# The first batch's prologue in two halves of the heads, its loads issued in another order, in a fused attention and feed-forward kernel

## The chip, the cores and the metric

The kernel runs on one core of a Trainium2 chip. The metric is the device time of one execution in microseconds (us). Engines are called as in the profile: PE (TensorE matmuls) and PEld (its weight loads), DVE (VectorE), ACT (ScalarE), POOL, SP; SPq and ACTq are the instruction queues of SP and ACT where they issue transfers (DMAs).

## The reference

For 8 batches of 8 heads (576 positions, head width 64) the keys and values are first summed into 32 memory slots per head, with softmax weights over the slots; the queries then attend to these 32 slots; the result, 4608 rows of 512, passes a two-layer feed-forward net with 2048 hidden units. All is float32, and the two weight matrices arrive as float64 words.

```python
a = softmax(phi)                        # over the 32 slots; phi: (8, 8, 576, 32)
k_m = einsum('bhsm,bhsd->bhmd', a, k)
v_m = einsum('bhsm,bhsd->bhmd', a, v)
attn = softmax(q @ k_m.T / 8)           # over the 32 slots
x = (attn @ v_m) as (4608, 512)
h = x @ w_in
out = (h * sigmoid(h)) @ w_out
```

## The kernel before

**The work of a batch.** Heads are laid out as two groups of four: group p (0 or 1), written g in tile layouts, takes columns or partitions 64 p to 64 p + 63 of a tile, and r (0 to 3) runs over the four heads of a group. A batch takes `phi` (loaded as `e`, 4 full chunks of 128 positions, and `er`, the last 64), subtracts the maximum, takes the exponential, multiplies it onto keys and values (`e_mm`; the tile `kv{c}` is chunk c, `kr` the last 64 positions; a column of ones gives the softmax sum beside), divides (`kvn`), transposes (`f_tr`, into `kvT`), and multiplies the keys with the queries (`f_scores`). The scores are copied (`f_copy`), turned by PE so that the slots lie along the free axis (`f_turn`), and go through maximum, subtraction, exponential, sum, reciprocal and product (`f_max`, `f_sub`, `f_exp`, `f_sum`, `f_norm`). They are turned back (`f_back`) and split into a rounded high part and the rest (`f_high`, `f_low`), so that matmuls in the fast float32 format keep the precision. The values are multiplied into `w_in` beforehand (`p_mm`, split by `p_split`), so that the hidden layer is one product of attention weights with this matrix (`ffn1`). Then come silu, a split and the second layer (`main_step`), for 16 chunks of 128 hidden units.

**The weights in the first batch.** They arrive as 64-bit words (`w_load`, 512 KB a half). `w_conv` makes float32 of them in steps: `p` and `c` on ACT (L172, L174), `s` and `a` on DVE (L176, L178), and for `w_out` `h` on ACT (L180) and `l` on DVE (L182). I0, O0 and I1 are the first chunks of `w_in`, `w_out` and the second of `w_in`; I0 and O0 come in two halves, 0 and 1.

**The order of the work.** The prologue of batch 0 is written out by hand (L1153 to L1251). Inside it PE, DVE, ACT and SP each run their instructions in the order in which the code names them. `keep_warm` adds matmuls without use so that PE is not idle. Behind the prologue a table of events puts each step at a slot of a chunk; the change does not touch that table, and the order of each engine behind the prologue is as it was.

**The halves before.** `f_scores(u)`, `f_copy(u)` and `f_turn(u)` work on half u of the query positions (288 each) for all eight heads; so both halves need the whole `kvT`, and with it all keys and values. Maximum to split then run for `u = 0`, `u = 1`, and the leftover 64 positions go with `u = 1`.

**The loads before.** `load_phi(0)` issues two parts on SP and one on ACT, 576 KB together. ACT then issues the four chunks of `kv` (516 KB each) and `kr` (258 KB); SP issues I0's first half, the two query halves (576 KB each), I0's second half, O0, I1 and the next weights. On SP every load from the first of I0 on is made to wait for the landing of the load that stands `DEEP = 5` places ahead in the code (`few=True`).

**The counters.** Each load reports its landing on one of eight counters, DMAHW0 to DMAHW7, which the framework hands out in turn in the order in which its scheduler places the loads. A load that gets a counter which another holds waits, in the queue of its engine, until that other load has landed.

Of the kernel before, what the change touches and what calls it, by code (L numbers as in the profile page):

```python
# [10 lines left out]
F32 = mybir.dt.float32  # L11
# [8 lines left out]
P = 128  # L20
# [6 lines left out]
CW = 256  # L27
# [21 lines left out]
def attn_ffn_kernel(  # L49
# [179 lines left out]
    def load_kv(b, cs=range(FULLC)):  # L229
        queue = nc.scalar if b == 0 else None  # L230
        ts = at[b].setdefault("kv", [])
        for c in cs:
            tag = f"q{c - 2}" if b > 2 and c > 1 else f"kv{c}"
            t = sb.tile([P, 2, NR, KVW], F32, tag=tag, name=f"kv{b}_{c}", bufs=1)
            load(t.rearrange("p g r f -> p (g r f)"), kv[b, :, c * KVC : (c + 1) * KVC], queue=queue)
            ts.append(t)
        if cs[0]:
            return
        t = sb.tile([P, NR, KVW], F32, tag="kr", name=f"kr{b}", bufs=1)
        load(t.rearrange("p r f -> p (r f)"), kv[b, :, FULLC * KVC :], queue=queue)  # L240
# [243 lines left out]
    first = {}  # L484
    UW = (2 * HM, 2 * HM + P)

    def f_tr():
        pt = ps.tile([P, 512], F32, tag="acc", name="firstt", bufs=NI)
        t = sb.tile([P, 2, NR, M], F32, tag="kvT", name="kvT0", bufs=2)
        at[0]["kvT"] = t  # L490
        for kind in range(2):
            nc.tensor.transpose(
                pt[:, P * kind : P * (kind + 1)], kvn[:, kind].rearrange("p g d -> p (g d)"), ident
            )
        nc.vector.tensor_copy(t[:, 0].rearrange("p r m -> p (r m)"), pt[:, :P])
        first["vt"] = t, pt

    def f_vt():
        t, pt = first["vt"]
        nc.scalar.copy(t[:, 1].rearrange("p r m -> p (r m)"), pt[:, P : 2 * P])  # L500

    def f_scores(u):
        if u == 0:
            t = [ps.tile([P, 512], F32, tag="acc", name=f"firsts{p}", bufs=NI) for p in range(2)]
        else:
            h = ps.tile([P, 2, 512], F32, tag="h", name="firsts", bufs=1)
            t = [h[:, p] for p in range(2)]
        kvT, q = at[0]["kvT"], at[0]["q", u]
        for r in range(NR):
            for p in range(2):  # L510
                nc.tensor.matmul(
                    t[p][M * r : M * (r + 1), :HALF],
                    kvT[D * p : D * (p + 1), 0, r],
                    q[D * p : D * (p + 1), r],
                    start=True, stop=True, skip_group_check=True,
                )
        first["st", u] = t if u == 0 else h

    def f_copy(u):
        if u == 0:  # L520
            first["left"] = sb.tile([P, P], F32, tag="mx", name="sleft", bufs=1)
        t = first["main", u] = sb.tile([P, 2, 2 * P], F32, tag=f"kv{u}", name=f"sT{u}", bufs=1)
        left = first["left"].rearrange("p (g h f) -> p g h f", g=2, h=2)[:, :, u]
        st = first["st", u]
        if u:
            nc.scalar.copy(t, st[:, :, : 2 * P])
            nc.scalar.copy(left, st[:, :, 2 * P : HALF])
# [36 lines left out]
    def f_max(u):  # L564
        nc.vector.tensor_reduce(
            f_part(u, "mx", 2 * S // M), f_groups(first["ps", u][:, : UW[u]]), op=ALU.max, axis=AX.X
        )

    def f_sub(u):
        nc.vector.tensor_tensor(  # L570
            f_groups(f_sc(u)), f_groups(first["ps", u][:, : UW[u]]), f_bc(f_part(u, "mx", 2 * S // M), u),
            op=ALU.subtract,
        )

    def f_exp(u):
        nc.scalar.activation(f_sc(u), f_sc(u), AF.Exp, scale=SCALE)

    def f_sum(u):
        sm = f_part(u, "sm", 2 * S // M)
        nc.vector.tensor_reduce(sm, f_groups(f_sc(u)), op=ALU.add, axis=AX.X)  # L580
# [22 lines left out]

    def f_to(x, u):
        v = at[0][x].rearrange("p g (h f) -> p g h f", h=2)
        return v[:, :, u, : 2 * P] if u < 2 else v[:, :, :, 2 * P :]

    def f_high(u):
        if "ahi" not in at[0]:
# [544 lines left out]
    with in_order(DVE, ACT) as last:  # L1154
        load_phi(0)
        nc.scalar.activation(tiny[:, :1], ident[:, :1], AF.Exp)
        load_kv(0)
        for c in LOADS.split():
            if c[0] == "Q":
                load_q(0, int(c[1]), True)  # L1160
            elif c[0] == "L":
                load_next(True)
            else:
                w_load((c[0], 0), int(c[1]), True)
        keep_warm(idle, 10)
        phi_max(0, (0,))
        phi_allmax(0, (0,))
        phi_max(0, (1,))
        keep_warm(idle, 3)
        phi_sub(0, (0,))  # L1170
        phi_allmax(0, (1,))
        phi_sub(0, (1,))
        for p in range(2):
            phi_exp(0, (p,))
        keep_warm(idle, 2)
        e_mm(0)
# [31 lines left out]
        w_conv(O0, 0, "c")
        keep_warm(spare, 3)
        bg = p_mm(0, 0, CW, False)  # L1210
        keep_warm(spare, 5)
        p_split(0, 0, CW, bg, (0,))
        w_conv(I1, None, "p")
# [7 lines left out]
        w_conv(O0, 0, "h")  # L1221
        f_low(1)
# [172 lines left out]
```

## Time and profile before

| | us |
|---|---|
| device time, median of 3 runs (lowest, highest) | 675.97 (675.60, 676.06) |
| the profiled execution's own time | 676.14 |
| its span, first to last instruction | 674.4 |
| PE busy | 664.5 |
| DVE busy | 518.7 |
| ACT busy | 370.2 |

So 1.74 us of the profiled execution lie outside its span. The times in the views count from the span's start. A row of the timeline gives the start and the length of a piece of work, the engine, the line in the code, the operation and its tiles, and in square brackets how long the engine was idle before and what ended that. A matmul of float32 operands shows as two records.

### The profile page before, as it was taken

To read this page: it belongs to the slowest core of one execution; us is meant where nothing else is said; L and a number is where in the kernel's file an instruction comes from. 1 tells how busy PE (TensorE), PEld (TensorE's weight loads), DVE (VectorE), ACT (ScalarE), POOL (GpSimd) and SP (SyncE) were. 2 spreads that over 40 slices of the span, in tenths; PEclk is the share of its full clock that TensorE was granted. 3 is DMA by queue.
4 is the path that set the end of the run, shared out by engine and by line. 5 is a ranking of instruction groups with operands and counts; after the bars stand their busy time and mean duration, and the time that the engine had idled before them with its cause. 6 is when DMAs were issued, how large, how long until landed. Compare 5 with 4: busy or idle time off the path is not lost.

```text
span 674.4 us, 14536 instructions
## 1 busy us (share of the span) xinstructions
PE 664.5 (99%) x5792; PEld 588.7 (87%) x5792; DVE 518.7 (77%) x1092; ACT 370.2 (55%) x686; POOL 0.7 (0%) x6
## 2 busy tenths in 40 slices
PE   7999999999999999999999999999999999999997
PEld 3588778887869998999988999899997999889996
DVE  3997899889958599878877688877877667867653
ACT  3878684534545556654645546564654646554441
POOL 0000000000000000000000000000000000000000
PEclk9999999999999999999999999999999999999999
DMA  9989985225251562253420534216430304300001
GB/s 340 366 329 298 313 308 184 91 92 172 93 188 38 185 205 79 79 201 131 153 94 17 185 121 163 69 47 229 157 126 33 87 2 157 115 27 18 32 1 48
DMA packets 37907, 93.92 MB, mean 139 GB/s; under 512 B 4688, under 2 KB 21456, under 8 KB 34256
## 3 DMA queue, kind: packets, MB, share of 16 engines
q1 hardware_dynamic: 36816, 90.22, 38.6%
q10 hardware_dynamic: 1024, 2.77, 1.1%
q8 instruction: 46, 0.75, 0.5%
q14 instruction: 21, 0.17, 0.1%
HBM read 77.22 MB, written 15.73 MB: 138 GB/s over the span
## 4 chain that ended last, share of the span: by engine, by line
PE 87%; DVE 2%; ACT 1%; issue 1%; DVEq 0%; ACTq 0%
PE sum L895 36%; PE h L856 23%; PE acc L746 9%; PE h L701 5%; PE lsum L979 5%; PE bg L649 3%; PE accleft L746 2%; PE bg L382 1%; PE h L335 1%; PE bg L335 1%; PE pacc L649 1%; DVE wf L814 0%; DVE kept L836 0%; ACT kept L835 0%; PE lsum L1001 0%
## 5 line engine op out<-in xcount | busy, mean ns | idle before, releaser
L856 PE MATMUL h<-aparts,pm 128*128 128x288 f32 x1152 | 168.5, 295 | 0.0
L856 PEld LDWEIGHTS h<-aparts,pm 128*128 128x128 f32 x1152 | 157.4, 189 | 0.5
L870 ACT ACTIVATE gbuf<-h 128x512 f32<-128x512 f32 x96 | 57.3, 597 | 117.1 <-PE h L856 113.8
L895 PE MATMUL sum<-wo_hi,aparts 128*128 128x256 f32 x384 | 102.4, 289 | 0.0
L895 PE MATMUL sum<-kept,aparts 128*128 128x256 f32 x576 | 100.2, 283 | 0.0
L895 PE MATMUL sum<-wo_lo,aparts 128*128 128x256 f32 x384 | 100.1, 282 | 0.0
L875 DVE TENSOR_TENSOR gbuf<-gbuf 128x256 f32<-128x256 f32 x96 | 40.6, 423 | 69.2 <-ACT gbuf L870 68.8
L884 ACT ACTIVATE aparts<-gbuf 128x512 fp32r<-128x512 f32 x86 | 54.4, 633 | 62.0 <-DVE gbuf L879 62.0
L895 PEld LDWEIGHTS sum<-kept,aparts 128*128 128x128 f32 x576 | 82.6, 191 | 0.0
L895 PEld LDWEIGHTS sum<-wo_hi,aparts 128*128 128x128 f32 x384 | 72.8, 190 | 9.8 <-ACT gleft L872 7.5
L886 DVE TENSOR_TENSOR gparts<-gbuf,aparts 128x512 fp32r<-128x512 f32 x86 | 59.6, 693 | 19.7 <-ACT aparts L884 19.6
L895 PE MATMUL sum<-wo_hi,gparts 128*128 128x256 f32 x384 | 73.2, 282 | 0.0
L895 PEld LDWEIGHTS sum<-wo_lo,aparts 128*128 128x128 f32 x384 | 73.2, 191 | 0.0
L746 PE MATMUL acc<-wo_hi,gparts 128*128 128x512 f32 x256 | 72.1, 395 | 0.0
L895 PE MATMUL sum<-kept,gparts 128*128 128x256 f32 x288 | 65.6, 282 | 0.0
L895 PEld LDWEIGHTS sum<-wo_hi,gparts 128*128 128x128 f32 x384 | 59.4, 190 | 0.0
L701 PEld LDWEIGHTS h<-aparts,pm 128*128 128x128 f32 x372 | 51.8, 188 | 6.3 <-issue 2.5
L701 PE MATMUL h<-aparts,pm 128*128 128x288 f32 x372 | 55.8, 299 | 0.5 <-DVE aparts L612 0.5
L746 PEld LDWEIGHTS acc<-wo_hi,gparts 128*128 128x128 f32 x256 | 46.1, 188 | 10.1 <-issue 1.0
L874 ACT ACTIVATE aparts<-gbuf 128x384 fp32r<-128x384 f32 x96 | 50.4, 525 | 0.0
L895 PEld LDWEIGHTS sum<-kept,gparts 128*128 128x128 f32 x288 | 47.9, 190 | 0.0
L885 DVE TENSOR_TENSOR gparts<-gbuf,aparts 128x384 fp32r<-128x384 f32 x86 | 47.4, 551 | 0.0
(226 smaller groups left out, 947.7 us busy)
## 6 DMA issues: line engine op xcount, KB each, us to landing
win<-win_saved SPq DMA_DIRECT2D x24, 1024.0 KB, 4.9
kv<-in_kv SPq DMA_DIRECT2D x28, 516.0 KB, 5.0
q<-in_q SPq DMA_DIRECT2D x16, 576.0 KB, 6.2
raw<-in_w_in SPq DMA_DIRECT2D x14, 512.0 KB, 7.8
raw<-in_w_out SPq DMA_DIRECT2D x6, 1024.0 KB, 6.9
win_saved<-win SPq DMA_DIRECT2D x4, 1024.0 KB, 8.7
phi<-in_phi SPq DMA_DIRECT2D x7, 576.0 KB, 8.0
out<-oo SPq DMA_DIRECT2D x26, 128.0 KB, 1.8
```

The costliest lines, as they stand in the source:

```text
L649: nc.tensor.matmul((bg[p][M * r : M * (r + 1)] if beside else bg[M * r : M * (r + 1), p, :w]).rearrange("p (k f) -> p k f", f=P), kvT[D * ...
L701: nc.tensor.matmul(h[:, hf, :HALF], wt[:, p, fs], a[:, p, hf * HALF : (hf + 1) * HALF], start=n[hf] == 0, stop=n[hf] == 5, skip_group_chec ...
L746: nc.tensor.matmul(acc[key], gt[:, cs], wt[:, fc], start=fc == 0 and n == 0, stop=fc == NFC - 1 and n == 2)
L856: nc.tensor.matmul(h[:, i, :HALF], wt[:, p, f : f + P], a[:, p], start=n == 0, stop=n == 5)
L870: nc.scalar.activation(gbuf[:, :MAIN].rearrange("p (i f) -> p i f", i=2), h[:, :, :w], AF.Silu)
L874: nc.scalar.activation(hi[:, :3], g[:, 1:4], AF.Copy)
L875: nc.vector.tensor_tensor(g[:, 4:6], g[:, :1].broadcast_to([P, 2, P]), g[:, 1:3], op=ALU.subtract)
L884: nc.scalar.activation(hi[:, 3:], g[:, 4:], AF.Copy)
L885: behind(nc.vector.tensor_tensor(lo[:, :3], g[:, 1:4], hi[:, :3], op=ALU.subtract).ins, s4)
L886: last_split.append(nc.vector.tensor_tensor(lo[:, 3:], g[:, 4:], hi[:, 3:], op=ALU.subtract))
L895: nc.tensor.matmul(sums[bank][:, place * Q : (place + 1) * Q], gt[:, k], wt, start=bank not in begun, stop=True, skip_group_check=True,)
L979: nc.tensor.matmul(sums[k], part[gt][:, 2 * i + k], wt[:, fc], start=n == 0 and i == 0 and m == 0, stop=True, skip_group_check=True,)
```

## The change

- **Loads.** `load_kv0(g)` and `load_q0(g)` load keys and values, and the queries, of one group of heads: 258 KB for a chunk of `kv`, 129 KB for `kr` and 288 KB for a half of the positions of `q`. Group 0 of `kv` goes on ACT's queue, all the rest on SP's. The code names `kv` of group 0, `q` of group 0, `kv` of group 1, I0's first half, `q` of group 1, I0's second half, and then the other weights as before. Only I0's second half and what follows it is still tied to the landing of an earlier load by `few`.
- **Order of computing.** The new `f_sums(p)` and `f_div(p)` take the place of `e_mm(0)` for the two groups one after the other. `f_tr`, `f_vt`, `f_scores`, `f_copy` and `f_turn` now work on one group of heads for all query positions. Group 0 is turned, and group 1 summed, before the maximum of group 0.
- **Softmax.** `f_sum` holds only the sums; `f_rec` takes the reciprocal of both halves together. `f_norm(0)` stands behind `f_sum(1)`.
- **Conversions.** I0's first half is converted behind `f_sub(0)`, its second `s` and `a` ahead of `f_sum(1)`, `p_mm(0, 0)` moves ahead of `f_norm(0)`, and I1's step `p` behind O0's `h`.
- **Buffers.** The copied scores lie in `gbuf` and not in the first two `kv` tiles.

```diff
+    def load_kv0(g, few=False):
+        queue = None if g else nc.scalar
...
+        for c in range(FULLC):
+            f = c * KVC + g * n
+            load(at[0]["kv"][c][:, g].rearrange("p r f -> p (r f)"), kv[0, :, f : f + n], few, queue)
+        load(at[0]["kr"][rows(g)].rearrange("p r f -> p (r f)"), kv[0, rows(g), FULLC * KVC :], few, queue)
...
+    def f_sums(p):
...
+        for c in range(FULLC):
+            for r in range(NR):
+                nc.tensor.matmul(
+                    pt[M * r : M * (r + 1), :KVW],
+                    e[:, p, c, M * r : M * (r + 1)],
+                    kvt[c][:, p, r],
+                    start=c == 0, stop=False, skip_group_check=True,
+                )
...
+    def f_div(p):
+        pt = first["pt", p]
+        rs = sb.tile([P, 1], F32, tag="rs", name="rs", bufs=2)
+        nc.vector.tensor_scalar(rs, pt[:, 2 * D : KVW], EPS, None, op0=ALU.add)
+        nc.vector.reciprocal(rs, rs)
+        src = pt[:, : 2 * D].rearrange("p (k d) -> p k d", k=2)
+        nc.vector.tensor_scalar(kvn[:, :, p], src, rs, None, op0=ALU.mult)
...
-        load_kv(0)
-        for c in LOADS.split():
...
+        load_kv0(0)
+        load_q0(0)
+        load_kv0(1)
+        w_load(I0, 0)
+        load_q0(1)
+        w_load(I0, 1, True)
...
-        e_mm(0)
-        w_conv(I0, 0, "pc")
-        keep_warm(idle, 3)
-        f_tr()
-        f_vt()
-        w_conv(I0, 0, "s")
-        keep_warm(idle, 2)
-        f_scores(0)
-        f_scores(1)
-        f_copy(0)
-        w_conv(I0, 0, "a")
-        f_turn(0)
-        f_copy(1)
-        f_max(0)
-        f_turn(1)
-        f_sub(0)
+        f_sums(0)
+        f_div(0)
+        keep_warm(idle, 3)
+        f_tr(0)
+        f_vt(0)
+        keep_warm(idle, 1)
+        f_scores(0)
+        f_copy(0)
+        keep_warm(idle, 1)
+        f_sums(1)
+        f_div(1)
+        f_turn(0)
+        f_tr(1)
+        f_vt(1)
+        f_max(0)
+        f_sub(0)
+        w_conv(I0, 0, "pc")
+        keep_warm(idle, 4)
+        f_scores(1)
+        f_exp(0)
+        w_conv(I0, 0, "sa")
+        f_copy(1)
+        f_turn(1)
         spare = ps.tile([P, 512], F32, tag="acc", name="spare", bufs=NI)
-        keep_warm(spare, 3)
-        f_exp(0)
+        keep_warm(spare, 6)
         w_conv(I0, 1, "pc")
+        f_sum(0)
         f_max(1)
         f_sub(1)
         f_exp(1)
         nc.scalar.activation(tiny[:, :1], ident[:, :1], AF.Silu)
-        keep_warm(spare, 13)
-        f_sum(0)
+        w_conv(I0, 1, "sa")
+        bg = p_mm(0, 0, CW, False)
+        keep_warm(spare, 3)
+        f_sum(1)
+        f_rec()
         f_norm(0)
-        w_conv(I0, 1, "sa")
         f_back(0)
-        f_sum(1)
...
```

How the rows of the engines stand, at three places. First ACT's own queue at the start, before (the names in square brackets are what a row waits for; `kv_c` is chunk c):

```order
L88 DMA kv_0_101<-in_kv 128x1032
L88 DMA kv_1_103<-in_kv 128x1032
L88 DMA kv_2_105<-in_kv 128x1032
L88 DMA kv_3_107<-in_kv 128x1032
L88 DMA kr_109<-in_kv 128x516 [waits DMAHW1_49]
L322 ACTIVATE phi_96<-phi_96 128x512 [waits DVE_49]
```

The same place now, where these are the loads of group 0:

```order
L88 DMA kv_0_101<-in_kv 128x516 [waits DMAHW2_49]
L88 DMA kv_1_102<-in_kv 128x516 [waits DMAHW4_49]
L88 DMA kv_2_103<-in_kv 128x516 [waits DMAHW5_49]
L88 DMA kv_3_104<-in_kv 128x516 [waits DMAHW7_49]
L88 DMA kr_105<-in_kv 64x516 [waits DMAHW0_49]
L342 ACTIVATE phi_96<-phi_96 128x512 [waits DMAHW1_49,DVE_49]
```

Each of the five loads of group 0 has become half as large, and each of them now waits for a counter, where one of five did. They stand ahead of the exponential of `phi` (L322, now L342) in the same queue, as before.

SP's queue at the start, now (`phi`, then queries and keys; `raw` are weights):

```order
L88 DMA phi_96<-in_phi 128x512
L88 DMA phi_96<-in_phi 128x128
L88 DMA q_0_111<-in_q 64x1152
L88 DMA q_1_113<-in_q 64x1152
L88 DMA kv_0_101<-in_kv 128x516
L88 DMA kv_1_102<-in_kv 128x516
L88 DMA kv_2_103<-in_kv 128x516
L88 DMA kv_3_104<-in_kv 128x516 [waits DMAHW0_49]
L88 DMA kr_105<-in_kv 64x516 [waits DMAHW1_49]
L88 DMA raw<-in_w_in 128x4x128 [waits DMAHW3_49]
L88 DMA q_0_111<-in_q 64x1152 [waits DMAHW6_49]
L88 DMA q_1_113<-in_q 64x1152 [waits DMAHW1_49]
```

Counters 1 to 7 go to the first seven of these rows in turn, counter 0 to the `phi` part on ACT; the eighth and ninth row take 0 and 1 again. ACT's five loads got theirs behind these: the counters that they wait for are held by the small `phi` part (2), `q_1` of group 0 (4), and `kv_0` (5), `kv_2` (7) and `kv_3` (0) of group 1. Before, SP's queue held, behind `phi`, I0's first half, which waited for the first `kv` chunk.

DVE before, from the division to the maximum of half 1 (`rs` and `kvn` divide, `fmx` and `fsc` are `f_max` and `f_sub`; L176 and L178 convert I0's first half):

```order
L353 TENSOR_SCALAR rs<-first_168 128x1
L353 TENSOR_SCALAR rs<-first_169 128x1
L355 RECIPROCAL rs<-rs 128x1 x2
L361 TENSOR_SCALAR kvn<-first_168,rs 128x2x64
L495 COPY kvT_224<-firstt 128x128
L176 TENSOR_SCALAR win_72<-win_72 128x512
L530 COPY sT_252<-firsts_233 128x256
L178 ISA win_72<-raw,win_72 128x1024
L565 TENSOR_REDUCE fmx<-firstu 128x16
L570 TENSOR_TENSOR fsc<-firstu,fmx 128x512
L565 TENSOR_REDUCE fmx<-firstu 128x20
```

DVE now, from the division of group 1 on:

```order
L529 TENSOR_SCALAR rs<-first_226 128x1
L530 RECIPROCAL rs<-rs 128x1
L532 TENSOR_SCALAR kvn<-first_226,rs 128x2x64
L544 COPY kvT_204<-firstt 64x128
L614 TENSOR_REDUCE fmx<-firstu 128x16
L619 TENSOR_TENSOR fsc<-firstu,fmx 128x512
L176 TENSOR_SCALAR win_72<-win_72 128x512
L178 ISA win_72<-raw,win_72 128x1024
L628 TENSOR_REDUCE fsm<-fsc 128x16
L614 TENSOR_REDUCE fmx<-firstu 128x20
```

I0's two conversion steps and `f_sum(0)` (L628) now stand between the maximum of half 0 and that of half 1, and a second division and a second copy of `kvT` stand ahead of both.

More of the change, by code (lines that the diff above doesn't have):

```diff
@@ L241, in load_kv, with load_q0 @@
         at[b]["kr"] = t
+    def load_kv0(g, few=False):
+        queue = None if g else nc.scalar
+        if g == 0:
+            at[0]["kv"] = [
+                sb.tile([P, 2, NR, KVW], F32, tag=f"kv{c}", name=f"kv0_{c}", bufs=1) for c in range(FULLC)
+            ]
+            at[0]["kr"] = sb.tile([P, NR, KVW], F32, tag="kr", name="kr0", bufs=1)
+        n = NR * KVW
+        for c in range(FULLC):
+            f = c * KVC + g * n
+            load(at[0]["kv"][c][:, g].rearrange("p r f -> p (r f)"), kv[0, :, f : f + n], few, queue)
+        load(at[0]["kr"][rows(g)].rearrange("p r f -> p (r f)"), kv[0, rows(g), FULLC * KVC :], few, queue)
+    def load_q0(g, few=False):
+        for hf in range(2):
+            if g == 0:
+                at[0]["q", hf] = sb.tile([P, NR, HALF], F32, tag=f"q{hf}", name=f"q0_{hf}", bufs=1)
+            d = slice(D * g, D * (g + 1))
+            load(at[0]["q", hf][d].rearrange("p r s -> p (r s)"), qT[0, hf, d], few)
     def load_q(b, hf, few=False):
@@ L485, in attn_ffn_kernel @@
     UW = (2 * HM, 2 * HM + P)
-    def f_tr():
+    def f_sums(p):
+        e, er, kvt, kr = (at[0][k] for k in ("e", "er", "kv", "kr"))
+        pt = first["pt", p] = ps.tile([P, 512], F32, tag="acc", name=f"first{p}", bufs=NI)
+        for c in range(FULLC):
[6 more added lines that the diff above has]
+                )
+        for r in range(NR):
+            nc.tensor.matmul(
+                pt[M * r : M * (r + 1), :KVW],
+                er[rows(p), M * r : M * (r + 1)],
+                kr[rows(p), r],
+                start=False, stop=True, skip_group_check=True,
+            )
@@ L488, in f_tr @@
+    def f_div(p):
[5 more added lines that the diff above has]
+        nc.vector.tensor_scalar(kvn[:, :, p], src, rs, None, op0=ALU.mult)
+    def f_tr(p):
         pt = ps.tile([P, 512], F32, tag="acc", name="firstt", bufs=NI)
-        t = sb.tile([P, 2, NR, M], F32, tag="kvT", name="kvT0", bufs=2)
@@ L490, in f_tr @@
-        at[0]["kvT"] = t
+        if p == 0:
+            at[0]["kvT"] = sb.tile([P, 2, NR, M], F32, tag="kvT", name="kvT0", bufs=2)
+        t = at[0]["kvT"]
+        d = slice(D * p, D * (p + 1))
         for kind in range(2):
-            nc.tensor.transpose(
-                pt[:, P * kind : P * (kind + 1)], kvn[:, kind].rearrange("p g d -> p (g d)"), ident
-            )
[L495 to L500, printed above, removed]
+            nc.tensor.matmul(
+                pt[d, P * kind : P * (kind + 1)], kvn[:, kind, p], ident, start=True, stop=True, skip_group_check=True
+            )
@@ L502, in f_scores, with f_vt @@
+        nc.vector.tensor_copy(t[d, 0].rearrange("p r m -> p (r m)"), pt[d, :P])
+        first["vt", p] = t[d, 1], pt[d, P : 2 * P]
+    def f_vt(p):
+        t, pt = first["vt", p]
+        nc.scalar.copy(t.rearrange("p r m -> p (r m)"), pt)
     def f_scores(u):
         if u == 0:
-            t = [ps.tile([P, 512], F32, tag="acc", name=f"firsts{p}", bufs=NI) for p in range(2)]
+            t = [ps.tile([P, 512], F32, tag="acc", name=f"firsts{hf}", bufs=NI) for hf in range(2)]
         else:
@@ L506, in f_scores @@
             h = ps.tile([P, 2, 512], F32, tag="h", name="firsts", bufs=1)
-            t = [h[:, p] for p in range(2)]
-        kvT, q = at[0]["kvT"], at[0]["q", u]
+            t = [h[:, hf] for hf in range(2)]
+        d = slice(D * u, D * (u + 1))
         for r in range(NR):
-            for p in range(2):
+            for hf in range(2):
                 nc.tensor.matmul(
-                    t[p][M * r : M * (r + 1), :HALF],
-                    kvT[D * p : D * (p + 1), 0, r],
-                    q[D * p : D * (p + 1), r],
+                    t[hf][M * r : M * (r + 1), :HALF],
+                    at[0]["kvT"][d, 0, r],
+                    at[0]["q", hf][d, r],
@@ L521, in f_copy @@
             first["left"] = sb.tile([P, P], F32, tag="mx", name="sleft", bufs=1)
-        t = first["main", u] = sb.tile([P, 2, 2 * P], F32, tag=f"kv{u}", name=f"sT{u}", bufs=1)
-        left = first["left"].rearrange("p (g h f) -> p g h f", g=2, h=2)[:, :, u]
+        t = first["main", u] = gbuf.rearrange("p (g h f) -> p g h f", g=2, h=2)[:, u]
+        left = first["left"].rearrange("p (g h f) -> p g h f", g=2, h=2)[:, u]
         st = first["st", u]
@@ L578, in f_sum, with f_rec @@
     def f_sum(u):
-        sm = f_part(u, "sm", 2 * S // M)
-        nc.vector.tensor_reduce(sm, f_groups(f_sc(u)), op=ALU.add, axis=AX.X)
+        nc.vector.tensor_reduce(f_part(u, "sm", 2 * S // M), f_groups(f_sc(u)), op=ALU.add, axis=AX.X)
+    def f_rec():
+        sm = first["sm"]
         nc.vector.tensor_scalar(sm, sm, EPS, None, op0=ALU.add)
@@ L605, in f_to @@
         v = at[0][x].rearrange("p g (h f) -> p g h f", h=2)
-        return v[:, :, u, : 2 * P] if u < 2 else v[:, :, :, 2 * P :]
+        return v[:, u, :, : 2 * P] if u < 2 else v[:, :, :, 2 * P :]
     def f_high(u):
@@ L1156, in attn_ffn_kernel @@
         nc.scalar.activation(tiny[:, :1], ident[:, :1], AF.Exp)
-        load_kv(0)
-        for c in LOADS.split():
[L1159 to L1164, printed above, removed]
+        load_kv0(0)
[4 more added lines that the diff above has]
+        w_load(I0, 1, True)
+        w_load(O0, 0, True)
+        w_load(O0, 1, True)
+        for _ in range(3):
+            load_next(True)
         keep_warm(idle, 10)
@@ L1199, in attn_ffn_kernel @@
         nc.scalar.activation(tiny[:, :1], ident[:, :1], AF.Silu)
-        keep_warm(spare, 13)
-        f_sum(0)
+        w_conv(I0, 1, "sa")
[3 more added lines that the diff above has]
+        f_rec()
         f_norm(0)
-        w_conv(I0, 1, "sa")
         f_back(0)
-        f_sum(1)
         w_conv(O0, 0, "p")
+        p_split(0, 0, CW, bg, (0,))
+        w_conv(O0, 0, "c")
         f_high(0)
[L1208 to L1213, printed above, removed]
         f_norm(1)
@@ L1221, in attn_ffn_kernel @@
         w_conv(O0, 0, "h")
+        w_conv(I1, None, "p")
         f_low(1)
```

## The prediction

> **What bounds the kernel now.** The windows come first:
>
> ```profile
> core 0: us, PE busy (x) PEld busy (x) DVE busy (x) ACT busy (x) POOL busy (x), PEclk, DMA share, GB/s
> 5.00:10.00 5.00, 3.84 (x37) 1.84 (x35) 3.42 (x10) 1.10 (x3) 0.00 (x0) 1.00 1.02 398
> 10.00:15.00 5.00, 4.19 (x87) 1.99 (x79) 1.42 (x8) 2.31 (x7) 0.00 (x0) 1.00 1.05 384
> 25.00:30.00 5.00, 4.31 (x30) 3.85 (x30) 5.00 (x11) 4.08 (x7) 0.00 (x0) 1.00 1.10 355
> 30.00:35.00 5.00, 5.00 (x41) 3.80 (x40) 4.28 (x8) 4.78 (x8) 0.00 (x0) 1.00 0.76 300
> ```
>
> From 30 us on PE is never idle; ahead of that it waits, and its busy time there contains the matmuls without use. So the prologue is the only part that this change can shorten or lengthen, and a shift of its end should reach the end of the kernel, since every engine's order behind it is unchanged. Two things work in the prologue: the transfers, saturated at 384 to 398 GB/s, and a chain of compute. The waits up to 17 us show which transfers are waited for:
>
> ```profile
> DVE mt L258 <- DMA phi<-in_phi: 4.1, 1, 4.1
> PE firsts L511 <- DMA q<-in_q: 0.8, 1, 0.8
> PEld first L345 <- DMA kr<-in_kv: 0.2, 1, 0.2
> ```
>
> Behind 17 us the same view names no transfer. So the loads set when the sums of keys and values end, and from there on the compute chain goes. The timeline has that chain:
>
> ```profile
> 8.61 0.29 ACT L323 ACTIVATE phi<-phi 64x128 f32<-64x128 f32 x1
> ...
> 9.34 0.87 PE L335 MATMUL first<-kv,phi 128*32 128x129 f32 x24
> ...
> 10.59 1.31 PE L335 MATMUL first<-kv,phi 128*32 128x129 f32 x40 [0.39 <-DMA kv<-in_kv]
> ...
> 11.83 0.45 PE L345 MATMUL first<-kr,phi 64*32 64x129 f32 x16
> ...
> 13.21 0.66 ACT L172 ACTIVATE win<-raw 128x512 f32<-128x512 f32 x1
> ...
> 13.76 0.68 ACT L174 ACTIVATE raw<-raw 128x512 int32<-128x512 uint32 x1
> 13.84 0.29 DVE L495 COPY kvT<-firstt 128x128 f32<-128x128 f32 x1 [0.67 <-PE firstt L492]
> ...
> 14.05 0.42 DVE L176 TENSOR_SCALAR win<-win 128x512 uint32<-128x512 uint32 x1
> ...
> 14.19 0.72 PE L511 MATMUL firsts<-q,kvT 64*32 64x288 f32 x16
> 14.32 0.26 ACT L500 COPY kvT<-firstt 128x128 f32<-128x128 f32 x1
> ...
> 15.38 0.68 DVE L178 CUSTOM_DVE_ANT_0 win<-raw,win 128x1024 uint16<-128x1024 uint16 x1
> ...
> 16.50 0.59 ACT L526 COPY sT<-firsts 128x512 f32<-128x512 f32 x1 [0.82 <-PE firsts L511]
> 16.98 0.22 ACT L527 COPY sleft<-firsts 128x64 f32<-128x64 f32 x1
> 17.03 0.69 DVE L565 TENSOR_REDUCE fmx<-firstu 128x16 f32<-128x512 f32 x1 [0.97 <-PE firstu L543]
> ...
> 17.25 0.66 PE L543 MATMUL firstu<-ident,sT 128*128 128x128 f32 x4 [0.26 <-ACT sleft L527]
> ...
> 17.75 0.27 PE L545 MATMUL firstu<-ident,sleft 128*128 128x128 f32 x1
> ...
> 17.76 0.69 DVE L570 TENSOR_TENSOR fsc<-firstu,fmx 128x512 f32<-128x512 f32 x1
> ...
> 18.37 0.81 DVE L565 TENSOR_REDUCE fmx<-firstu 128x20 f32<-128x640 f32 x1
> 18.48 0.63 ACT L576 ACTIVATE fsc<-fsc 128x512 f32<-128x512 f32 x1 [1.28 <-DVE fsc L570]
> ...
> 19.96 0.68 DVE L580 TENSOR_REDUCE fsm<-fsc 128x16 f32<-128x512 f32 x1
> ...
> 20.15 0.72 ACT L576 ACTIVATE fsc<-fsc 128x640 f32<-128x640 f32 x1
> ...
> 21.16 0.69 DVE L586 TENSOR_TENSOR fsc<-fsc,fsm 128x512 f32<-128x512 f32 x1
> ...
> 22.29 0.67 ACT L172 ACTIVATE cva<-raw 128x512 f32<-128x512 f32 x1
> ...
> 22.87 0.58 ACT L614 ACTIVATE aparts<-firsta 128x512 fp32r<-128x512 f32 x1
> ...
> 23.98 0.60 ACT L677 ACTIVATE pm<-bg 128x512 fp32r<-128x512 f32 x1
> ...
> 25.04 0.69 DVE L617 TENSOR_TENSOR aparts<-firsta,aparts 128x512 fp32r<-128x512 f32 x1
> ...
> 27.45 0.28 DVE L617 TENSOR_TENSOR aparts<-firstar,aparts 128x128 fp32r<-128x128 f32 x1
> ```
>
> From the maximum at 17.03 on DVE hardly pauses until the last split ends at 27.73 (27.45 + 0.28). That split frees the first `ffn1`, and so all that follows. I call the landing of `kr` T, and the start of the second half's maximum (18.37) Y; from Y to the last split are 9.36 us.
>
> **The loads, part by part.** The number of bytes stays. What moves is who comes first. These rows are the issues of before, with KB each and us to landing (the last from a window of 5.5 to 6.5 us):
>
> ```profile
> kr<-in_kv ACTq DMA_DIRECT2D x1, 258.0 KB, 7.6
> raw<-in_w_in SPq DMA_DIRECT2D x1, 512.0 KB, 6.9
> ```
>
> ```profile
> 4.11 0.34 ACTq L88 DMA_DIRECT2D kr<-in_kv  x1
> ...
> 5.75 0.39 SPq L88 DMA_DIRECT2D raw<-in_w_in  x1
> ```
>
> So `kr` landed at 4.11 + 7.6 = 11.7 us, with 2898 KB asked for up to it (phi 576, kv 2064, kr 258). In the new order SP asks at once for the queries of group 0 and keys and values of group 1, and ACT's loads of group 0, which are needed first, wait for counters: the first for the small part of phi, the second for `q_1`, the third, fourth and fifth for `kv_0`, `kv_2` and `kv_3` of group 1. So the loads do wait for landings, and those needed first come last. The last, `kr` of group 0, is asked for only when `kv_3` of group 1 has landed: phi 576 + q 576 + four chunks 1032 = 2184 KB, and one chunk of ACT's own in between, 2442 KB or 2.50 MB; kr's case (2.97 MB, 11.7) less 0.47 MB at 390 GB/s gives 10.5, without the mixing there about 9.2.
>
> For the new T there are two bounds. If ACT's loads keep pace and nothing of the weights goes ahead, 576 + 576 + 1161 + 1161 = 3474 KB lie up to it: 576 KB or 0.59 MB more than before, 1.5 us at 390 GB/s, which gives 13.2; but `kr` of before had part of the 512 KB behind it mixed in (issued 1.64 us later, landed at 12.65, 0.95 later), at most 0.52 MB or 1.3 us, so 12.0 is the lower end. If I0's first half (asked for when `q_0` has landed) and one query half (288 KB) go ahead as well, 4274 KB or 4.38 MB less the mixing give 11.7 - 1.3 + 1.41/0.39 = 14.0, the upper end. Loads of 64 rows do not occur in the prologue of before; at half the rate the 705 KB of them ahead of T would add 1.8 us, at the same rate nothing. I take 13.3, nearer the upper end, because kr and the raw load show that SP's later load does hold back ACT's.
>
> [...]
>
> ACT stands still at its waiting loads until about 9.2, and the exponential of phi is queued behind them (8.61 + 0.29 = 8.90 was its end for group 0). With T at 13.3 that costs nothing; without the late loads it would.
>
> **From T to Y.** Before, T to the scores took 14.19 - 11.7 = 2.5. Half the last sums (0.45 / 2) and one division for two leave 2.2; the scores take 0.72: T + 2.9. One warming matmul, then the sums of group 1: half of 0.87 + 1.31 + 0.45 is 1.3, up to T + 4.45 (group 1's data are there by then). Division, transposition and copy took from 12.28 (11.83 + 0.45) to 14.13 (13.84 + 0.29), 1.85; one division less leaves 1.65: T + 6.1. On DVE the maximum and subtraction of half 0 follow, 17.03 to 18.45 before, so 1.42: T + 7.6. On ACT meanwhile the copy of kvT (0.26) and I0's p and c (0.66 + 0.68) end at T + 7.7; then the exponential (0.63, T + 8.3), the copies of the second scores (16.50 to 17.20, 0.7, T + 9.0), and PE turns them (17.25 to 18.02, 0.77). With handovers of 0.05 each Y = T + 9.95. Before it was T + 6.7 (18.37 - 11.7): the halves now follow each other where they shared the sums, the division and the transposition.
>
> **From Y on.** `f_sum(0)` with its reciprocal (19.96 to 21.16, 1.2 us) has gone ahead of Y, which leaves 9.36 - 1.20 = 8.16. But `f_low(0)`, at 25.04 - 18.37 - 1.20 = Y + 5.47 for DVE, now waits for ACT: O0's p starts at Y + 3.92 as before (22.29), then p, pm, c and `f_high(0)` (0.67 + 0.60 + 0.68 + 0.58, 2.4 with their overlaps) end at Y + 6.3. That adds 0.8. The last split ends at Y + 8.96. I1's p and c, now behind O0's h on ACT, hold the first silu by up to 0.4; I take 0.3. The removed warming matmuls cost and bring nothing: PE waits there.
>
> **Sum.** 13.3 + 9.95 + 8.96 + 0.3 - 27.73 = 4.8 us later. Against the profiled execution's 676.14 that is 680.9; the median is 0.17 lower, so **680.8** in round numbers. The ends of T give 3.5 to 5.5, so 679.4 to 681.5, and with slow 64-row loads 683.3.
>
> **The rivals.**
> - *The loads are prompt.* ACT's waits are satisfied in time and group 0 lands as it is consumed. Then phi's exponential bounds: matmuls from 9.34 on, 1.3 us for group 0, whose end at 10.64 corresponds to T = 10.25 (the last sums end 0.4 behind T). That is 3.05 less than 13.3, so 1.75 later than before: 677.7. For it: half the bytes serve group 0. Against it: the counters above.
> - *Faster.* The loads are prompt, and besides the sums, division and transposition of group 1 hide under group 0's copies (1.65 us), so that the maximum of half 0 starts at T + 4.45 = 14.7. From there DVE, without a pause, needs the 10.7 us of before (17.03 to 27.73), I0's two steps more (0.42 + 0.68) and one reciprocal pair less (21.16 - 20.64 = 0.5), 11.3: the last split ends at 26.0, and the kernel takes 674.2. It decides below a maximum at 16.4, where 11.3 gives 27.7. For it: that maximum needs half the heads alone. Against it: on DVE it stands behind group 1's copy of kvT, and with prompt loads alone it starts at 16.35, which gains nothing.
> - *Absorbed.* Work behind the prologue has slack, and the delay vanishes: 676.0. Against it PE's 5.00 of 5.00.
> - *PE's clock drops.* PE would have little to do from 9.4 until T. If its clock halved, its rows between T and Y that lie on the chain (0.23 + 0.72 + 1.3 + 0.77) would add about 3.0: 683.8. PEclk is 1.00 in every window here, and PE had no such pause, so the trace bears out little. [...]
>
> **How the numbers follow.** My forecast has 0.63, prompt loads 0.17, the clock 0.06, absorbed 0.06, faster 0.08. The range 677.3 to 683.3 leaves out faster, absorbed and the clock, 0.2; its lower end gives the prompt case 0.4 for what the chain may overlap further. A measurement tells 0.2% (1.35 us) from no change: slower 0.79, the first three cases less 0.07 of the prompt one, whose size may come out within; same 0.13, that and absorbed; faster 0.08.
>
> **What would show it.** Right: `f_sums(0)` on PE waits for transfers until about 13.3, L342 on ACT starts past 9, Y near 23, the last split near 32, PE full behind it. Wrong: the first scores start before 13 (loads prompt), Y - T is much under 9.95 (chain), or PE shows new waits past 35 us. A median under 677 makes the whole argument wrong.

## The result, and the profile after

| us | before | after |
|---|---|---|
| device time, median (lowest, highest) | 675.90 (675.60, 676.06) | 690.53 (689.36, 692.88) |
| the profiled execution's own time | 676.14 | 689.36 |
| its span | 674.4 | 687.6 |
| PE busy | 664.5 | 669.5 |
| DVE busy | 518.7 | 519.6 |
| ACT busy | 370.2 | 370.5 |

The changed kernel takes 1.0219 times as long, with a 95% interval of 1.0205 to 1.0232: 14.6 us more in the medians, 13.2 in the profiled executions. That is the direction of the forecast and three times its size. PE is busy for 5.0 us longer although it computes the same products: some of it ran at a lower clock, 0.50 from 15 to 20 us. These are the windows of the changed kernel, with the columns of the prediction's first fence:

```profile
5.00:10.00 5.00, 2.82 (x13) 1.20 (x11) 3.65 (x11) 0.00 (x0) 0.00 (x0) 1.00 1.02 293
10.00:15.00 5.00, 1.14 (x16) 0.41 (x16) 0.00 (x0) 1.65 (x4) 0.00 (x0) 0.64 1.09 314
15.00:20.00 5.00, 3.28 (x31) 0.89 (x27) 0.67 (x3) 0.00 (x0) 0.00 (x0) 0.50 1.06 270
...
30.00:35.00 5.00, 2.88 (x27) 0.89 (x24) 4.54 (x8) 3.54 (x6) 0.00 (x0) 1.00 0.36 100
35.00:40.00 5.00, 3.88 (x16) 3.34 (x17) 3.98 (x9) 4.04 (x7) 0.00 (x0) 0.53 0.85 303
```

The last column has fallen from 398 and 384 GB/s to 293 and 314, and 270 behind that, while the DMA share beside it still says that all engines are busy. The third column from the right, PE's clock, was 1.00 throughout before; it is 0.64 and 0.50 between 10 and 20 us, and 0.53 from 35 to 40. Both were sizes that the prediction had put aside. The load of `kr` for group 0, from the issues of the changed kernel between 11.5 and 12.5 us:

```profile
kr<-in_kv ACTq DMA_DIRECT2D x1, 129.0 KB, 6.2
```

And its timeline, cut to the chain (on the row of a wait, the brackets name what ended it):

```profile
4.99 5.59 ACTq L88 DMA_DIRECT2D kv<-in_kv  x4
...
11.86 0.54 ACTq L88 DMA_DIRECT2D kr<-in_kv  x1
12.51 0.63 ACT L342 ACTIVATE phi<-phi 128x512 f32<-128x512 f32 x1 [9.83 <-DMA kr<-in_kv]
...
13.19 0.66 PE L512 MATMUL first<-kv,phi 128*32 128x129 f32 x8 [3.99 <-ACT phi L342]
...
16.70 0.66 PE L512 MATMUL first<-kv,phi 128*32 128x129 f32 x8 [1.52 <-DMA kv<-in_kv]
...
18.15 0.65 PE L519 MATMUL first<-kr,phi 64*32 64x129 f32 x8
...
21.71 1.19 PE L560 MATMUL firsts<-q,kvT 64*32 64x288 f32 x16
...
24.18 0.42 PE L519 MATMUL first<-kr,phi 64*32 64x129 f32 x8
...
26.54 0.69 DVE L614 TENSOR_REDUCE fmx<-firstu 128x16 f32<-128x512 f32 x1
...
30.20 0.82 DVE L614 TENSOR_REDUCE fmx<-firstu 128x20 f32<-128x640 f32 x1 [0.49 <-PE firstu L594]
...
38.25 3.22 PE L752 MATMUL h<-aparts,pm 128*128 128x288 f32 x12 [0.94 <-DVE aparts L663]
...
39.21 0.28 DVE L668 TENSOR_TENSOR aparts<-firstar,aparts 128x128 fp32r<-128x128 f32 x1
...
41.57 0.60 ACT L779 ACTIVATE gbuf<-h 128x512 f32<-128x512 f32 x1 [0.84 <-PE h L752]
```

ACT's queue held `kr` back until 11.86; it landed 6.2 us later, so T, its landing, is 18.0. Y, the start of the second maximum, is 30.20, the last split ends at 39.49, and the first silu, with which the steady part begins, starts at 41.57. The two rows of before that this is to be held against, the first hidden layer and its silu:

```profile
26.48 2.10 PE L701 MATMUL h<-aparts,pm 128*128 128x288 f32 x12 [0.47 <-DVE aparts L612]
...
28.62 0.60 ACT L728 ACTIVATE gbuf<-h 128x512 f32<-128x512 f32 x1 [0.49 <-PE h L701]
```

The first silu is 12.95 us late and the end of the span 13.2: the delay arises ahead of the steady part and is passed on whole.

### The profile page after: what moved, and what is told of

It reads as the page before. It is cut to its first block, busy times and chain, and to the rows that moved or that the text cites. A ratio compares the mean times of both kernels' runs of the same rounds, so it can differ in the third digit from the quotient of the medians.

```text
span 687.6 us, 14530 instructions
## 1 busy us (share of the span) xinstructions
PE 669.5 (97%) x5787; PEld 591.6 (86%) x5787; DVE 519.6 (76%) x1092; ACT 370.5 (54%) x686; POOL 0.7 (0%) x6
## 4 chain that ended last, share of the span: by engine, by line
PE 85%; DVE 2%; ACT 1%; issue 1%; DVEq 0%; ACTq 0%
PE sum L946 36%; PE h L907 22%; PE acc L797 9%; PE h L752 5%; PE lsum L1030 5%; PE bg L700 3%; PE accleft L797 2%; PE bg L402 1%; PE bg L355 1%; PE h L355 1%; PE pacc L700 1%; DVE wf L865 0%; DVE kept L887 0%; ACT kept L886 0%; PE lsum L1052 0%
```

## The experiments

Each diff is against the kernel that is named with it. The theory: three things add up, loads that come late, a clock that drops while PE waits, and the longer chain of two groups. The rival: the loads alone account for nearly all of it.

**The two halves of the change apart.** `old_loads`, against the changed kernel: its order of computing with the loads of before.

```diff
-        load_kv0(0)
-        load_q0(0)
-        load_kv0(1)
-        w_load(I0, 0)
-        load_q0(1)
...
+        load_kv(0)
+        for c in LOADS.split():
...
```

> The changed kernel's computing with the loads of before, in size and order. Theory of the late loads (the landing of the last keys and values of group 0 moved from 11.7 to 18.0 us, and PE's pause there cost it the clock): that landing goes back to about 11.7, PEclk stays 1.00 up to 30 us, and 2 to 4 us over before remain for the computing by groups, 678 to 680. Rival, the computing by groups costs most by itself: 685 or more. Rival, the clock alone: as near to before as 676 to 677, since PE's early pause is gone.

`new_loads`, against the kernel before: its order of computing with the new loads.

```diff
...
-        load_kv(0)
-        for c in LOADS.split():
...
+        load_kv0(0)
+        load_q0(0)
+        load_kv0(1)
+        w_load(I0, 0)
+        load_q0(1)
...
```

> The computing of before with the changed kernel's loads. Theory of the late loads: the last keys and values land near 18 us, ACT's first exponential starts past 12, the clock falls near 11.5 us as in the changed kernel; 6.3 us for the landing and 1 to 3 for the clock, 683 to 686. Rival, the computing by groups costs most by itself: 676 to 678.

Measured: 683.95 us, ratio 1.0111 (1.0094 to 1.0128), and 684.12 us, 1.012 (1.0105 to 1.0135). By these ratios the order of computing alone costs 7.5 us and the loads alone 8.1, so the loads aren't nearly all, and the order of computing costs more than the 678 to 680 us that I had expected. For it, this is the timeline of `old_loads`:

```profile
14.83 1.19 PE L560 MATMUL firsts<-q,kvT 64*32 64x288 f32 x14 [0.81 <-DMA q<-in_q]
...
16.50 1.95 PE L512 MATMUL first<-kv,phi 128*32 128x129 f32 x32
...
32.77 3.22 PE L752 MATMUL h<-aparts,pm 128*128 128x288 f32 x12 [0.97 <-DVE aparts L663]
```

The scores of a group need both halves of its queries, so they wait for the second query load, which the first scores of before don't need. The sums of group 1, queued behind these scores on PE, come late and at a lower clock (0.66 from 15 to 20 us; 1.95 us for the keys, where the changed kernel needs 1.09 at a clock of 1.00), and the hidden layer takes 3.22 us for 2.10 (0.50 from 30 to 35). How the 7.5 us divide among these, no run shows.

**The queue.** `kv_on_sp`, against the changed kernel: group 0's keys and values go on SP's queue, directly behind `phi` and ahead of the queries, with no wait.

```diff
-        queue = None if g else nc.scalar
+        queue = None
```

> The changed kernel with the keys and values of group 0 issued by SP too, ahead of all else but phi; each load of group 0 is then issued without a wait. Theory of the late loads: group 0 lands by about 9 to 10 us, the first sums end near 10.5, and 1 to 3 us over before remain, 677 to 679. Rival, the halved loads are slow wherever they stand in the queue: group 0 lands past 11 and the kernel takes 681 or more.

Measured: 681.78 us, ratio 1.0081 (1.0066 to 1.0096), 8.75 us less than the changed kernel. The edit takes the waits away and puts these loads first in the order; the run doesn't separate the two. Its timeline:

```profile
9.07 1.09 PE L512 MATMUL first<-kv,phi 128*32 128x129 f32 x32
...
19.93 0.64 PE L560 MATMUL firsts<-q,kvT 64*32 64x288 f32 x2 [1.01 <-DMA q<-in_q]
...
21.06 1.19 PE L560 MATMUL firsts<-q,kvT 64*32 64x288 f32 x14 [0.48 <-DMA q<-in_q]
...
24.47 0.82 DVE L614 TENSOR_REDUCE fmx<-firstu 128x20 f32<-128x640 f32 x1 [2.99 <-PE firstu L594]
```

Sums start at 9.07 where they started at 13.19. The time is in the range of the rival all the same, and not because group 0 is late. The wait has moved on: now the queries of group 1, last in the order, hold the second scores until 21.06.

`act_whole_q`, against the changed kernel: the queries come in whole loads of 128 partitions, where those of group 0 stood, and ACT's queue still waits.

```diff
-        load_q0(0)
+        load_q(0, 0)
+        load_q(0, 1)
...
-        load_q0(1)
```

> The changed kernel with its queues, but the queries in two loads of 128 rows (576 KB each) where those of group 0 stood, and none for group 1. ACT's loads of group 0 wait for counters as in the changed kernel. Theory that both the waits and the slow 64-row loads made the last keys and values of group 0 late: they land near 15 instead of 18, ACT's exponential starts near 11 instead of 12.5, and the kernel takes 686 to 688. Rival, the waits alone: still 18, and 690. Rival, the 64-row loads alone: near 12, and 682.

Measured: 691.83 us, ratio 1.0235 (1.022 to 1.025), no better than the change, although the transfers run faster (382, 328, 341 GB/s in the windows from 5 to 20 us). I had expected 686 to 688. From its timeline and windows:

```profile
11.93 0.54 ACTq L88 DMA_DIRECT2D kr<-in_kv  x1
...
18.86 0.66 PE L519 MATMUL first<-kr,phi 64*32 64x129 f32 x8 [0.36 <-DMA kr<-in_kv]
...
22.42 2.17 PE L560 MATMUL firsts<-q,kvT 64*32 64x288 f32 x16
```

```profile
15.00:20.00 5.00, 2.49 (x30) 0.91 (x27) 0.36 (x3) 0.00 (x0) 0.00 (x0) 0.50 1.05 341
20.00:25.00 5.00, 5.00 (x25) 1.57 (x22) 0.89 (x3) 0.59 (x3) 0.00 (x0) 0.50 1.07 378
```

The faster transfers bring more bytes ahead of the same waiting queue (all 1152 KB of queries and more of I0), so `kr`, asked for at 11.93, lands at 18.72, no earlier than in the changed kernel. In this order, then, the 64-partition query loads are not by themselves what makes `kr` late. And PE's clock is 0.50 in both windows, so that the scores take 2.17 us for 1.19.

`sp_whole_q`, against the changed kernel: both edits together.

```diff
-        queue = None if g else nc.scalar
+        queue = None
...
-        load_q0(0)
+        load_q(0, 0)
+        load_q(0, 1)
...
-        load_q0(1)
```

> The changed kernel's computing with all first loads on SP in the order of use (keys and values of group 0, queries, keys and values of group 1, weights), the queries in loads of 128 rows. Theory of the loads (waits and slow 64-row loads): group 0 lands near 9, the queries near 12, group 1 near 14, no later wait for a transfer; what remains over before is the computing by groups alone, 2 to 4 us, 678 to 680. Rival, computing by groups costs as much as with the loads of before (8 us): 682 or more.

Measured: 680.55 us, ratio 1.0065 (1.0052 to 1.0079). Against `kv_on_sp` that is 1.2 us less, with intervals that overlap; Y comes at 22.15 where it was 24.47.

**What makes the loads slow.** `q_halves`, against the kernel before: nothing but the two query loads cut by partitions, two of 64 in place of each one of 128.

```diff
+        if b == 0:
+            for d in (slice(0, D), slice(D, P)):
+                load(t[d].rearrange("p r s -> p (r s)"), qT[b, hf, d], few)
+            return
```

> The kernel before with each of its two query loads (128 rows, 576 KB) cut into two loads of 64 rows at the same place in SP's queue; the same bytes, and nothing of the computing moved. Theory that loads of 64 rows run at about half the rate: a packet of 4608 bytes takes about 0.32 us for 0.18, the rate between 11 and 16 us falls to 200 to 280 GB/s for 384, the second queries land near 18 for 15.55, and the kernel takes 678 to 680. Rival, halved loads are as fast: 676.

`q_cols`, against the kernel before: the same cut by columns, so 128 partitions, the same size of 288 KB and the same number.

```diff
+        if b == 0:
+            for c in (slice(0, 2 * HALF), slice(2 * HALF, 4 * HALF)):
+                load(t.rearrange("p r s -> p (r s)")[:, c], qT[b, hf, :, c], few)
+            return
```

> The kernel before, with each of its two loads of queries cut by columns into two loads of 128 partitions and 288 KB (128x576), where the earlier run cut them by partitions into two of 64 partitions and 288 KB. Number, bytes and place of the loads are the same in both. Theory (64 partitions are what is slow): the rate in the windows from 10 to 20 us stays at 360 GB/s or more, the maximum of the second half starts within 0.6 us of 18.37, and the time is 676.0 to 676.8. Rival (the number or the size of the loads, or the wait of each for a counter, is what is slow): the windows show 270 to 310 GB/s again, the maximum starts near 21, and the time is 679 to 681.5.

Measured: 681.51 us, ratio 1.008 (1.0063 to 1.0096), for the cut by partitions; 676.24 us, 1.0009 (0.9999 to 1.0019), for the cut by columns. The transfers between 10 and 20 us in cells of a quarter of a microsecond, `q_halves` first (share of the DMA engines in tenths, then GB/s):

```profile
DMA  9999999999989999899999999999999999999999
GB/s 361 369 365 377 426 358 215 174 188 221 221 221 276 221 203 258 221 276 221 203 240 240 262 193 170 209 215 227 201 262 307 356 402 381 397 426 393 426 393 459
```

```profile
GB/s 336 332 361 345 350 404 396 386 387 406 415 387 387 396 396 400 336 343 373 332 360 365 381 283 283 262 328 377 361 410 426 377 410 303 291 307 328 307 303 389
```

In the first, from 11.5 to about 17 us, the rate is 222 GB/s on average, with about 400 behind it and the DMA engines busy all the while; in the second it is 363 over the same stretch. So the 64 partitions are what is slow here, at 222 GB/s, and not the number, the size or the counters of the loads. Why a load over 64 partitions is slower, no run shows.

The cut by partitions took longer than the 678 to 680 us expected. Its four executions fall in two pairs: 679.9 and 680.5 us with a mean clock of 0.999, and twice 682.5 or more with a clock of 0.994 to 0.995. So a part of the cost may lie with the clock.

**The clock.** `more_warm`, against the changed kernel: more matmuls without use while PE waits for group 0 (the four numbers are those behind each chunk of its sums) and ahead of the second softmax.

```diff
-        keep_warm(idle, 2)
-        f_sums(0)
+        keep_warm(idle, 20)
+        f_sums(0, (4, 8, 3, 1))
...
-        keep_warm(spare, 6)
+        keep_warm(spare, 13)
```

> The changed kernel with matmuls without use in PE's two long pauses (20 for 2 ahead of the first sums, 16 between its chunks, 13 for 6 behind the second turn). The loads stay late. Theory of the late loads with the clock as a part: PEclk stays 1.00, the landing stays near 18.0, and the kernel gains 2.5 to 3.5 us, 687 to 688. Rival, the clock is the bulk: 680 or less. Rival, the clock costs nothing on the chain: 690.

Measured: 688.76 us, ratio 1.0191 (1.0176 to 1.0206), 1.8 us less than the changed kernel. PE's clock is 1.00 in every window. Its timeline:

```profile
21.51 1.20 PE L561 MATMUL firsts<-q,kvT 64*32 64x288 f32 x16
...
30.01 0.82 DVE L615 TENSOR_REDUCE fmx<-firstu 128x20 f32<-128x640 f32 x1 [0.49 <-PE firstu L595]
...
37.68 2.10 PE L753 MATMUL h<-aparts,pm 128*128 128x288 f32 x12 [1.13 <-DVE aparts L664]
```

In this execution `kr` landed at 18.78, 0.76 later, yet the hidden layer, back at 2.10 us, ends 1.7 earlier. From T to Y it takes 11.23 us instead of 12.18.

`old_loads_warm` does the same against `old_loads`, ahead of the first scores and of the second softmax:

```diff
-        keep_warm(idle, 1)
+        keep_warm(idle, 8)
...
-        keep_warm(spare, 6)
+        keep_warm(spare, 13)
```

> The changed kernel's computing with the loads of before, and matmuls without use in the two pauses in which the clock fell there (8 for 1 ahead of the first scores, 13 for 6 behind the second turn). Theory that computing by groups costs by a longer chain and the clock adds to it: PEclk 1.00 throughout, 680 to 682, so 2 to 3.5 us less than with those loads alone and 4 to 6 over before. Rival, the clock was all of it: 676 to 677. Rival, the clock cost nothing: 684.

`whole_q_warm` does it against `sp_whole_q`, the last line behind `f_back(1)`:

```diff
-        keep_warm(spare, 6)
+        keep_warm(spare, 13)
...
-        keep_warm(spare, 3)
+        keep_warm(spare, 6)
...
+        keep_warm(spare, 4)
```

> The whole-query kernel on SP with more matmuls without use behind the second turn (13 for 6), ahead of the turning back (6 for 3) and ahead of the first hidden chunk (4 for 0). Theory that the clock's fall near 27 us lengthens the first hidden chunk (3.2 us for 2.1): PEclk stays 1.00 and 1 to 1.5 us are gained, 679 to 679.6. Rival, the fall costs nothing because DVE and ACT set the pace there: 680.5.

Measured: 682.33 us, ratio 1.0087 (1.0072 to 1.0103), and 679.34 us, 1.0054 (1.0037 to 1.007): 1.6 and 1.2 us less than without. The intervals overlap with those without, so these two gains are not sure from the times alone. In the first the clock still fell for the hidden layer (3.19 us; 0.997 on average over the profiled execution), in the second it did not (1.000).

**The slower scores.** The 16 score records of one group take 1.20 us even at a clock of 1.00; 16 of both groups took 0.72 before. A theory was that the order makes the difference: before, the two groups took turns. `scores_by_group`, against the kernel before, runs the four heads of one group and then those of the other:

```diff
-        for r in range(NR):
-            for p in range(2):
+        for p in range(2):
+            for r in range(NR):
```

> The kernel before with the two loops of the first scores exchanged, so that the matmuls of group 0 stand together and then those of group 1, as in the changed kernel, and not in turn. Theory that matmuls of the two groups (64 rows each) ran side by side and those of one group don't: the 16 records take 1.2 us for 0.72, twice on the chain at most, and the kernel takes 676.4 to 677. Rival, the order within does not matter and the 1.2 us of the changed kernel are something else: 676.

`scores_by_half`, against `sp_whole_q`, exchanges the loops over heads and query halves:

```diff
-        for r in range(NR):
-            for hf in range(2):
+        for hf in range(2):
+            for r in range(NR):
```

> The whole-query kernel on SP (sp_whole_q, 680.55) with the loops of the first scores exchanged: the four heads of a group for one half of the queries, then for the other. Two matmuls in a row then don't use the same 64 x 32 place of the array. Theory that only such neighbours wait for each other: the 16 records take 0.7 to 0.9 us for 1.2, and 0.3 to 0.8 us are gained, 679.8 to 680.2. Rival, a group's scores have four places where before there were eight, and the order among them does not matter: 1.2 us as before, 680.5.

Measured: 675.98 us, ratio 1.0 (0.9992 to 1.0009), and 679.74 us, 1.0063 (1.0047 to 1.0078). The scores of the first and then of the second:

```profile
14.00 0.72 PE L511 MATMUL firsts<-q,kvT 64*32 64x288 f32 x16
```

```profile
12.67 1.17 PE L560 MATMUL firsts<-q,kvT 64*32 64x288 f32 x16
```

The order makes next to no difference (1.17 us for 1.20), and that theory falls. That the second run is 0.8 us faster than `sp_whole_q` is not from the scores; the intervals overlap. The rows show 1.17 to 1.20 us for 16 records of one group, and 0.72 for 16 of both; why was only argued and stays open.

**What is left.** `groups_best`, against `scores_by_half`, adds the warming matmuls of `whole_q_warm`:

```diff
-        keep_warm(spare, 6)
+        keep_warm(spare, 13)
...
-        keep_warm(spare, 3)
+        keep_warm(spare, 6)
...
+        keep_warm(spare, 4)
```

> Both of the last two edits together: loads in order of use on SP, whole queries, scores by halves, PE kept busy. What is left over before is then the computing by groups. Theory: group 1's sums end near 16.5 because its keys land near 16, the maximum of the second half starts near 21.5, the last split ends near 30.5, and the kernel takes 678.3 to 679. Rival, computing by groups costs nothing once loads and clock are right: 676.

Measured: 679.31 us, ratio 1.0051 (1.0036 to 1.0066). Its timeline:

```profile
15.41 0.42 PE L519 MATMUL first<-kr,phi 64*32 64x129 f32 x8
...
21.43 0.82 DVE L614 TENSOR_REDUCE fmx<-firstu 128x20 f32<-128x640 f32 x1 [0.49 <-PE firstu L594]
...
29.10 2.10 PE L752 MATMUL h<-aparts,pm 128*128 128x288 f32 x12 [0.27 <-DVE aparts L663]
```

With the queue, the clock and most of the 64-partition loads mended, the second maximum is still 3.1 us late (21.43 for 18.37). The sums of group 1 end at 15.83, where all sums ended at 12.28 before: the queries are now asked for ahead of the keys of group 1, and division and transposition are run twice. What each of these costs, no run shows.

`kr_on_sp`, against the kernel before, asks whether its own one waiting load on ACT, `kr`, cost anything:

```diff
-        load(t.rearrange("p r f -> p (r f)"), kv[b, :, FULLC * KVC :], queue=queue)
+        load(t.rearrange("p r f -> p (r f)"), kv[b, :, FULLC * KVC :])
```

> The kernel before, with the load of the last 64 positions of keys and values moved from ACT's queue to SP's, so that ACT's exponential of phi has no load with a wait ahead of it. Theory (the loads set when the sums of keys and values end, and the queries at 14.06 us set the scores): the exponential starts earlier, the scores do not, and the time is 675.4 to 676.4. Rival (the exponential behind ACT's waiting load is on the path before the change too): the sums end over 0.5 us earlier and the time falls under 675.2.

Measured: 675.39 us, ratio 0.9992 (0.9983 to 1.0002). The exponential starts at 7.83 instead of 8.07, the last sums at 11.88 instead of 11.83: it was not on the path. No version that was run is measurably faster than the kernel before.

## Why the prediction was wrong in size

Held against its sum at the first silu, 4.8 us forecast and 12.95 measured:

| term | forecast | measured | miss |
|---|---|---|---|
| T, landing of `kr` of group 0 | 13.3 | 18.0 | +4.7 |
| T to Y | 9.95 | 12.2 | +2.2 |
| Y to the last split | 8.96 | 9.3 | +0.3 |
| last split to first silu | 1.2 | 2.1 | +0.9 |

- **The landing of `kr`: mechanism right, T too early.** That ACT's loads would wait for counters held by later ones, and that those needed first would come last, is what the ACT queue shows (issues from 4.99 to 11.86), and `kv_on_sp`, which undoes both, takes 8.75 us off. The step that failed is "I take 13.3"; measured is 18.0. The forecast counted bytes and left the rate of 64-partition loads as it was: "at half the rate the 705 KB of them ahead of T would add 1.8 us, at the same rate nothing". `q_halves` shows 222 GB/s, near half of the about 400 behind it, and `q_cols` 363. It had also to be joined to the upper end of the order, where one more query half of 288 KB and the second `kr` count among the 64-partition loads: 576 + 129 + 288 + 129 = 1122 KB or 1.15 MB, at half of 390 GB/s 2.9 us more, on top of 14.0. That estimate gives 16.9. Two bounds that can both come true were taken as alternatives. Of the other 1.1 us, 0.8 can be estimated: up to 18.02 the core had moved 4.70 MB (261 GB/s on average), 0.32 MB more than the 4.38 of the upper end, which takes 0.8 us at 390 GB/s.
- **The rate alone doesn't settle T.** In `act_whole_q` the query loads are fast, yet `kr` lands at 18.72, with 5.8 MB moved by then. What the two kernels share is the wait: `kr` is asked for at 11.86 and 11.93, and then needs 6.2 and 6.8 us to land. The prediction had it asked for at 9.2 to 10.5, and its own two rows show 7.6 and 6.9 us from issue to landing. Added up, these give 16.1 to 18.1, where 13.3 left 2.8 to 4.1 us for the flight. How much of the miss of 4.7 us is the rate and how much the late asking stays open: no run separates them.
- **Sharing between queues.** The forecast took 13.3 between its bounds because in the trace of before SP's load, issued 1.64 us behind ACT's, landed only 0.95 behind it. No run here tests that sharing in the new order, since ACT's loads were not yet asked for: the last stood in its queue until 11.86.
- **The phi exponential.** Forecast was that ACT stands until about 9.2 and that it costs nothing; it stood until 12.5. PE then had nothing to do for 3.99 us, and in that pause, at 11.42, its clock fell from 1.00 to 0.50.
- **The clock.** It had a chance of 0.06 and came true, twice. "PEclk is 1.00 in every window here, and PE had no such pause" was read from the trace of before, while the forecast itself put PE to waiting until T. That the clock would halve no row of before showed; the changed kernel shows 0.50. The price, 3.0 us between T and Y, was too high: `more_warm` shows 0.95 there; the clock was back at 21.66, before the first scores. A second drop, which the price didn't contain, costs 1.1 in the hidden layer (3.22 for 2.10, with 0.53 from 35 to 40 us). How busy PE was ahead of the falls is in the last section.
- **T to Y.** At a clock of 1.00 11.23 us remain against 9.95. The scores, set at 0.72, take 1.20; this was the row of the wrong shape, since before each 16 records went over both groups. That is 0.48 of the difference; about 0.55 lie ahead of the first scores (2.73 from T in `more_warm`, 2.18 forecast), and the remaining quarter of a microsecond was not taken apart.
- **What the forecast left out** is that a group's scores need both query loads. It did not bind here, with the queries early, but in `old_loads` and `kv_on_sp`.
- **From Y on** the sum held within 0.3 us up to the last split, and the claim that the shift reaches the end whole held as well. The prompt and the faster rival fall with T; nothing was absorbed.

The two halves of the change nearly add up: apart they cost 8.1 and 7.5 us, together 14.6.

## What to carry to other kernels

Before a load is cut, look at the number of partitions that each part covers: a cut by columns cost nothing measurable here, a cut into 64 partitions 0.8%, or 5.4 us. A load that is needed first must not stand in a queue where it waits for a counter that a later load holds; read which rows hold the counters, and what else is queued behind the waiting load. Behind such a wait, count the whole time from issue to landing, 6 to 7 us here for 129 KB, and not bytes alone. And when a forecast makes PE wait, its clock, which fell to 0.50 in such a wait here, belongs into the sum and not among the rivals.

## What the runs showed of the hardware

In the changed kernel PE's clock fell from 1.00 to 0.50 at 11.42 and 35.31 us and was back at 1.00 at 21.66 and 42.14: the distances are 10.24, 13.65 and 6.83 us, or 3, 4 and 2 times 3.41. The first fall came 2.2 us behind the end of PE's last matmul, and ahead of the second the longest pause was 1.63 us. These are that last matmul, that pause, and, nearly, the window that ended in the second fall:

```profile
8.60 0.59 PE L80 MATMUL idle<-ident 128*128 128x512 bf16 x2
```

```profile
33.09 0.67 PE L700 MATMUL bg<-win,kvT 64*32 64x256 f32 x16 [1.63 <-DVE win L178]
```

```profile
31.90:35.30 3.40, 1.54 (x20) 0.52 (x21) 3.17 (x7) 3.35 (x6) 0.00 (x0) 1.00 0.28 73
```

Cut into stretches of 3.41 us that end with a fall, the changed kernel had PE busy for 3.23, 2.31 and 0.92 us up to the first one, and for 3.41, 2.91, 2.06 and 1.55 from the return to the second. In other runs the fall can be placed to about 0.1 us by the clock of the windows, or by the rows around it. In the 3.41 us ahead of it PE was busy for about 0.6 us in `new_loads` (fall near 12.2), 1.7 in `act_whole_q` (10.7), 1.9 in `kv_on_sp` (22.3), 1.4 in `sp_whole_q` (26.9), and 2.2 and 1.4 in `old_loads` (15.9 and 29.6). So in none of these had PE been idle for the whole stretch, and the rows give no sharp limit: 2.2 us in `old_loads` ended in a fall, 2.06 in the changed kernel did not. With seven warming matmuls more behind the second turn the clock stayed at 1.00 in `more_warm` and fell in `old_loads_warm`: in the second they lie in a stretch with 3.29 us busy, and the next one, from 27.97 to 31.38, has 1.82; in the first PE was busy for 3.23, 2.45 and 2.28 us in the three stretches from 29.02 to 39.26.

A DMA share near 1 went with very different rates: 1.07 at 234 GB/s in `kv_on_sp` from 15 to 20 us, 1.02 at 398 in the kernel before from 5 to 10.
